# Routing of the later two token groups among the first expert's w_out products, six pieces by group at the end

## The chip, the cores and the metric

One core of a Trainium2 chip runs the whole program in one launch. The metric is device microseconds of one execution. Five engines work side by side, each through its own instructions in order: PE (TensorE, matmuls), ACT (ScalarE), DVE (VectorE), POOL (GpSimd) and SP (SyncE), which here issues nearly every transfer. PEld is the loading of the matmuls' fixed operand.

## The reference, cut to what matters

```python
x = attention(q, k, v, omega)                 # 1152 tokens x 512, random features
h = x @ w_in                                  # 2048 hidden channels
g = h * np.clip(h + 3.0, 0.0, 6.0) / 6.0
x = g @ w_out                                 # 1152 x 512
logits = x @ w_gate                           # 8 experts
expert_idx = np.argmax(logits, axis=1)
...                                           # softmax; a token counts if its expert has had < 288 before it
h = np.maximum(np.einsum('ecd,edf->ecf', disp, w1), 0.0)
y = np.einsum('ecf,efd->ecd', h, w2)
out[i] = gate_w[i] * y[expert_idx[i], pos[i]] # for the tokens that are kept, else 0
```

q, k and the weights of the middle layer are float64 or float32 of random numbers; the result is 1152 x 512 float32.

## The kernel before

After the attention the tokens stand in three groups of 384 (g = 0, 1, 2) and the 2048 hidden channels in 16 pieces of 128 (f = 0 to 15). PE makes `h` for one piece and one group with 12 matmuls (`hidden_in`, L274); ACT and DVE make `g` of it (L278, L282), in one of eight buffers with the tag `g`; SP stores it to memory (`gall`, and `gfirst` for group 0).

The logits are not made from `g @ w_out`. For each f, `w_out` is multiplied by `w_gate` first (`fold_gate`: four transposes, L296, four matmuls, L303, and ACT's copy to `wog`, L306), and `logits` (L315) adds `wog` times `g` into one PSUM bank `lg`, one matmul for each group. The constant `TAIL` says for how many of the last f this goes by group: all of group 0 of those f comes first, then groups 1 and 2, so that the logits of group 0 end early.

Routing has two parts: p = 0 is group 0, p = 1 is groups 1 and 2. Its steps, by the planner's names: `lc` (ACT copies the logits, L328), `lt` (PE turns them, L337, L340), `best` (DVE, eight small operations, L386 to L405), `exp` (ACT, L410), `rk` (PE, ranks within each expert, L416 to L420), `kept` (DVE, L426 to L449), `cb` (PE, sums over tokens, L474), `cc` (DVE, eleven small operations, L477 to L508: which expert e, and from which token s on, a window of 288 consecutive tokens is to serve), `gate` (DVE, L455 to L459). SP then reads s (L511) and e (L513) into registers and waits for DVE at that, with all later transfers behind it in its queue. `Lm` stores the rows `meta` of expert and weight to memory (`mfirst`, `mall`; L464, L465: 8 bytes for each token), and `Lsm` loads the rows of a window back (L545).

The first choice serves one window of the first group and one expert, the second another window over all tokens; a last branch serves what would be left. For each window: 16 loads of `g` at the chosen token (`gw`, L541, 144 KB each, in the same eight buffers), a split of each into two halves (`gh` on ACT, L549, `gl` on DVE, L551: the remainder; four buffers), and 16 products with `w_out` (`Yw`, L558, 12 matmuls each, into four PSUM banks). The sum is split into two halves (`th`, ACT, L568, and `tl`, DVE, L570: tile `dT`). Then the expert: eight loads of its weights (L590 for w1, L593 for w2: `rawe`, 512 KB each, four buffers), each for two splits (weight splits `wsplit`: `u`, ACT, L603; the remainder `v`, DVE or POOL, L605), eight products with w1 (`h0`, L626), products with w2, and the rows to the output.

The order on every engine is made by a planner (`Plan.order`): each step has an engine, a cost, what it comes after, which buffers it takes and frees, and a rank; the planner goes through time and gives each engine the step of lowest rank that could start. The program is then written in that order, and each engine keeps to it. Costs and ranks change nothing but this order. A wait on the chip is only one for data or for a buffer; of SP's transfers at most eight are under way, since the ninth waits for the first.

Of the kernel before, what the change touches and what calls it, by code (L numbers as in the profile page):

```python
# [10 lines left out]
F32 = mybir.dt.float32  # L11
# [120 lines left out]
def moe_kernel(ctx, tc, q, k, v, v_rest, omega, w_in, w_out, w_gate, w1, w2, out, cap):  # L132
# [6 lines left out]
    E, F2 = w2.shape[0], w2.shape[1]  # L139
    KD = DM // 128  # L140
    NG = 3
# [7 lines left out]
    F2T = F2 // 128  # L149
    F1T = FF // 128  # L150
# [10 lines left out]
    GB = 8  # L161
    WO0 = 4
# [3 lines left out]

    AHEAD = 4

    TAIL = 4
    H_TP = (1, 3, 5, 7)  # L170
    SPLITS = ["PDPDPDPDPDPDPDPD", "PDPDPDPDPDPDPDPD"]
    ABS_FROM = 12
# [11 lines left out]
    wa = ctx.enter_context(tc.tile_pool(name="wa", bufs=7))  # L184
    wo0 = ctx.enter_context(tc.tile_pool(name="wo0", bufs=WO0))
# [104 lines left out]
    wog = {}  # L290

    def fold_gate(f):
        wo = wtile["o", f].bitcast(F32)
        tp = pt.tile([128, KD, 128], F32, tag="tp", name="tpW")
        for kk in range(KD):
            nc.tensor.transpose(tp[:, kk, :], wo[:, kk * 128:(kk + 1) * 128], ident)  # L296
        yield
        woT = late_pools["woT"].tile([128, KD, 128], F32, tag="woT", name="woT")
        nc.scalar.activation(out=woT, in_=tp, func=ACTF.Copy)
        yield  # L300
        ps_ = late_pools["ac2"].tile([128, E], F32, tag="ac2", name="wogp")
        for kk in range(KD):
            nc.tensor.matmul(ps_, lhsT=woT[:, kk, :], rhs=wg[:, kk, :], start=(kk == 0), stop=(kk == KD - 1))  # L303
        yield
        wog[f] = late_pools["woT"].tile([128, E], F32, tag="wog", bufs=4, name="wog")
        nc.scalar.activation(out=wog[f], in_=ps_, func=ACTF.Copy)  # L306


    lg = []
# [16 lines left out]
    def logits_out(g):  # L326
        ps = slice(32 * g, 32 * g + E)
        nc.scalar.activation(out=lgT[0][ps], in_=lg[0][ps], func=ACTF.Copy)  # L328
# [3 lines left out]
    def turn_logits(p):  # L332

        lgr[p] = late_pools["ac2"].tile([128, len(PARTS[p]), E], F32, tag="ac2", name="lgr")
        if p == 0:
            for c in range(TPG):
                nc.tensor.transpose(lgr[p][:, c, :], lgT[0][0:E, c * 128:(c + 1) * 128], ident[0:E, 0:E])  # L337
            return
        for c in range(TPG):
            nc.tensor.matmul(  # L340
                lgr[p][:, c::TPG, :], lhsT=lgT[0][:, c * 128:(c + 1) * 128],
                rhs=ident.rearrange("p (g e) -> p g e", e=32)[:, 1:NG, 0:E], start=True, stop=True,
            )
# [524 lines left out]
    def turn_out(u):  # L868
# [31 lines left out]

    plan = Plan(dict(
        tp=4, pj=2, acc=1, x=XB, phi=3, phiR=1, phT=2, xo=2, nm=4, rd=4, x32=X32, raww=4, rawx=RAWX, rawv=2,
        t=2, g=GB, wa=7, wo0=WO0, wo=F1T - WO0 + 1, ohi=F1T, woT=2, wog=4, gh=4, wb=F2T - 1, g6k=2 * NG, yT2=2, lg=1, ac2=1,
    ), HOP, AGAIN, INTO, SLACK)

    def rank(stage, u):
# [41 lines left out]
    for u, (nm, b, c, hh) in enumerate(seq):  # L948
# [15 lines left out]
        for z in range(2):  # L964
# [4 lines left out]
                    after=[f"N{z}{u}"] + [f"P0{u}"] * z, takes=None if z else "phiR" if is_r else "phi",  # L969
                    frees=[f"B{z}{u}", f"N{z}{u}"], rank=rank("P", u))),  # L970
# [5 lines left out]
        after=[f"P0{ur}", f"P1{ur}", "VvR"] + [f"KR{x - 1}"] * (x > 0), takes="tp", frees=[f"P0{ur}"], rank=rank("K", ur))) for x in range(3)])  # L976
    chain(gen, [(f"KT{x}", "ACT", 0.46 if x < 2 else 0.37, dict(after=[f"KR{x}"] + [f"KT{x - 1}"] * (x > 0), frees=[f"KR{x}"], rank=rank("KV", ur))) for x in range(3)])
    for b in range(B):
        kus = [units["k", b, c, hh] for c in range(2) for hh in range(2)]
        names = []  # L980
        for u in kus:
            _, _, c, hh = seq[u]
            for z in range(2):
                name = f"K{b}.{u}.{z}"
# [3 lines left out]
                    after=[f"P{z}{u}", f"Vv{b}{c}"] + names[-1:], frees=[f"P0{u}"] + ([f"Lv{b}{c}"] if hh == 1 else []), rank=rank("K", u),  # L988
                    takes=None if names else "acc",
# [8 lines left out]
    for u, (nm, b, c, hh) in enumerate(seq):  # L998
        if nm != "q":
            continue  # L1000
        for z in range(2):
# [3 lines left out]
                    after=[f"C{z}{u}"] + [f"T0{u}"] * z, takes=None if z else "phT", frees=[f"C{z}{u}"], rank=rank("T", u))),  # L1005
            ])
        for z in range(2):
            chain(attend(u, z), [
                (f"D{z}{u}", "PE", 0.856, dict(
                    after=[f"T{z}{u}"] + [f"KV{bb}" for bb in range(B) if b in (bb, "R")], takes="tp",  # L1010
                    frees=[f"T0{u}"], rank=rank("D", u))),
# [11 lines left out]
    late_pools = {}  # L1023
# [37 lines left out]
    def load2(name, fn, cost, latency=0.95, **kw):  # L1061
        plan.add("L" + name, "SP", cost, fn, **kw)
        plan.add("V" + name, "in" + name, latency, lambda: None, after=["L" + name])
# [62 lines left out]
    for n, (_, f, g) in enumerate(order):  # L1126
        me = f"{f}.{g}"
        tag = "tp" if n % 2 else "pj"
# [15 lines left out]
    for f in range(F1T):  # L1144
        for gs in ([(0, 1, 2)] if f < F1T - TAIL else [(0,), (1, 2)]):
            plan.add(f"L{f}.{gs[0]}", "PE", 0.75, lambda a=(f, gs): logits(*a), after=[f"Hg{f}.{g}" for g in gs] + [f"Gc{f}o"] + ([] if first else ["L0.0"]),
                     takes="lg" if first else None, frees=[f"Hg{f}.{g}" for g in gs] + ([f"Gc{f}o"] if gs[-1] == NG - 1 else []), rank=pe_rank["L", f, gs[-1]])
# [3 lines left out]
        plan.named[f"L{f}.1"]["after"].append("lc0")  # L1151
    plan.add("lz", "Pool", 0.5, clear_logits, after=[f"WLi{F1T - 1}"], takes="x32", rank=0.0)
    for g in range(NG):
        plan.add(f"lc{g}", "ACT", 0.57, lambda g=g: logits_out(g), after=["lz", f"L{F1T - 1}.{min(g, 1)}"], frees=["L0.0"] if g else [], rank=-850)
    for p in range(2):
        plan.add(f"lt{p}", "PE", 0.2 if p else 0.1, lambda p=p: turn_logits(p), after=["lc1", "lc2"] if p else ["lc0"], takes="ac2", frees=["lz"] if p else [], rank=-800)


    for p in range(2):
        T = len(PARTS[p])  # L1160
        r = -800
        run_of(f"best{p}", route_best(p), [(0.1, [f"lt{p}"])] + [(0.094,), (0.094,), (0.094, 1), (0.094, 2), (0.094,), (0.094,), (0.081,)], r)
        plan.named[f"best{p}.0"]["frees"].append(f"lt{p}")
        plan.add(f"exp{p}", "ACT", 0.15, lambda p=p: route_exp(p), after=[f"best{p}.3"], rank=r)
        plan.add(f"rk{p}", "PE", 0.2 if p else 0.1, lambda p=p: route_rank(p), after=[f"best{p}.7"] + (["kept0.7"] if p else []), takes="ac2", rank=r)
        run_of(f"kept{p}", route_kept(p), [(0.094, [f"rk{p}"]), (0.094,), (0.07,), (0.07, 1), (0.094, 2), (0.094, 3), (0.07, 2)] + ([(0.094, None)] if not p else []), r)
        plan.named[f"kept{p}.0"]["frees"].append(f"rk{p}")
        gen = choose(p)
        chain(gen, [(f"cb{p}", "PE", 0.12, dict(after=[f"kept{p}.5"] + ([] if not p else ["cb0"]), takes="ac2", rank=r))])
        ops = [(0.1, [f"cb{p}"])] + [(0.08,)] * (9 + 2 * p)  # L1170
        run_of(f"cc{p}", gen, ops, r)
        plan.named[f"cc{p}.0"]["frees"].append(f"cb{p}")
        last = f"cc{p}.{len(ops) - 1}"
        chain(gen, [
            (f"cs{p}", "SP", 0.55, dict(after=[last], rank=-2000)),
            (f"ce{p}", "SP", 0.55, dict(after=[f"cs{p}"], rank=-1990 if p else -1950)),
        ])
        if p == 0:
            chain(gen, [("ct0", "DVE", 0.08, dict(after=[last], then=[last], rank=r))])
        run_of(f"gate{p}", route_gate(p), [(0.094, [f"exp{p}"]), (0.07,), (0.08,)], r + 50)  # L1180
        load2(f"m{p}", lambda p=p: save_meta(p), 0.5, 2.0, after=[f"gate{p}.2", f"kept{p}.6"], rank=-1940)
# [7 lines left out]
    for x, f in enumerate(YORDER):  # L1189
        prev = YORDER[x - 1]  # L1190
# [5 lines left out]
    def add_window(p, r):  # L1196
        x = windows[p]

        def load_meta():
            x.start = chosen[p]["st"]  # L1200
            x.load_meta()

        load2(f"sm{p}", load_meta, 0.5, 2.0, after=[f"cs{p}", f"Vm{p}"] + ([] if not p else ["Vm0"]), rank=-1930)
        run_of(f"to{p}", experts[p].target(), [(0.07, [f"Vsm{p}"]), (0.07,), (0.08,)], r + 40)
        for n, f in enumerate(YORDER):
            prev = f"{p}.{n - 1}" if n else f"{p - 1}.{F1T - 1}" if p else ""
            stored = [f"VHs{f}.{g}" for g in range(NG if p else 1)]
            load2(f"gw{p}.{n}", lambda f=f: x.load(f), 0.45, 2.0, after=[f"cs{p}"] + stored, takes="g", rank=-1980 + n + 400 * p, then=["Lgw" + prev] if prev else [])
            chain(x.halve(f), [
                (f"gh{p}.{n}", "ACT", 0.41, dict(after=[f"Vgw{p}.{n}"], takes="gh", rank=r + n, then=["gh" + prev] if prev else [])),  # L1210
                (f"gl{p}.{n}", "DVE", 0.45, dict(after=[f"gh{p}.{n}"], frees=[f"Lgw{p}.{n}"], rank=r + n)),
            ])
            plan.add(f"Yw{p}.{n}", "PE", 1.62, lambda f=f: x.product(f), after=[f"gl{p}.{n}", f"ol{f}"] + ([f"Yw{p}.{n - 1}"] if n else []),
                     takes=None if n else [("tp", f"yw{p}.{kk}") for kk in range(KD)], frees=[f"gh{p}.{n}"], rank=r + n)
        for kk in range(KD):
            chain(x.tokens(kk), [
                (f"th{p}.{kk}", "ACT", 0.33, dict(after=[f"Yw{p}.{F1T - 1}"] + ([f"th{p}.0"] if kk else []),
                                                  takes=None if kk else [("g6k", f"d{p}0"), ("g6k", f"d{p}1")], rank=r - 200)),
                (f"tl{p}.{kk}", "DVE", 0.38, dict(after=[f"th{p}.{kk}"], frees=[f"yw{p}.{kk}"], rank=r - 200)),
            ])  # L1220
# [187 lines left out]
```

## Time and profile before

| | us |
|---|---|
| median of three runs | 346.6 (345.59 to 346.85) |
| the profiled execution | 347.02 |
| its span, first to last instruction | 345.2 |
| PE busy | 328.8 (95% of the span) |
| DVE busy | 225.7 (65%) |
| ACT busy | 180.2 (52%) |

All times within the program are microseconds from the start of the span. The profiled execution spends 1.8 us outside its span. [...]

### The profile page before, as it was taken

How to read it: one execution, taken by the hardware profiler on the slowest of the kernel's cores; microseconds unless marked ns; L12 is line 12 of the kernel's file. 1: busy time of each engine (PE TensorE's matmuls, PEld its weight loads, DVE VectorE, ACT ScalarE, POOL GpSimd, SP SyncE). 2: the span in 40 equal slices, each digit the busy share in tenths (PEclk: the TensorE clock that was granted, in tenths of full speed). 3: DMA queues.
4: the chain of work that ended last, by engine and by line, in shares of the span. 5: the costliest groups of instructions: out<-in, count | busy, mean ns of one | idle time of the engine just before them, and what ended most of it. 6: DMA issues, size and time to landing. Idle time of an engine off the chain costs nothing.

```text
span 345.2 us, 6458 instructions
## 1 busy us (share of the span) xinstructions
PE 328.8 (95%) x2307; PEld 300.8 (87%) x2307; DVE 225.7 (65%) x465; ACT 180.2 (52%) x436; POOL 76.7 (22%) x74
## 2 busy tenths in 40 slices
PE   8998999999999999999999999599989999999992
PEld 5998899999888888888888778399889989999782
DVE  5489999899889899988884436377676202654100
ACT  6987999973345545554374622325646232624110
POOL 0846543100112121122000000013604212511021
PEclk9999999999999999999999999969999999999998
DMA  7996921013666867676322211858746004710011
GB/s 253 357 316 255 356 102 63 2 52 142 214 210 217 259 232 253 235 269 217 114 92 104 91 59 49 246 112 252 249 121 244 2 0 131 252 65 0 4 46 30
DMA packets 29674, 54.06 MB, mean 157 GB/s; under 512 B 5537, under 2 KB 18209, under 8 KB 29633
## 3 DMA queue, kind: packets, MB, share of 16 engines
q1 hardware_dynamic: 29248, 52.38, 45.9%
q0 software_dynamic: 384, 1.18, 1.1%
q8 instruction: 20, 0.33, 0.4%
q14 instruction: 22, 0.17, 0.2%
HBM read 37.42 MB, written 16.13 MB: 155 GB/s over the span
## 4 chain that ended last, share of the span: by engine, by line
PE 79%; issue 8%; DMA 4%; DVE 4%; ACT 2%; SPq 1%; POOL 1%; POOLq 0%; ACTq 0%; DVEq 0%
PE hp L274 30%; PE yw L558 10%; PE pj L776 6%; PE hp L626 6%; PE lg L315 5%; PE wogp L303 4%; PE yq L648 4%; PE nd L847 4%; PE kvp L799 3%; PE tpW L296 2%; PE tpC L829 2%; DMA rawe<-in_w_dram 2%; DMA out_dram<-scratch,to 2%; DMA rawx<-in_k_dram 1%; PE tpE L872 1%
## 5 line engine op out<-in xcount | busy, mean ns | idle before, releaser
L274 PE MATMUL hp<-xT,wsplit 128*128 128x384 f32 x576 | 112.5, 343 | 0.0
L274 PEld LDWEIGHTS hp<-xT,wsplit 128*128 128x128 f32 x576 | 98.0, 188 | 9.7 <-issue 8.4
L278 ACT ACTIVATE t<-hp,three 128x384 f32<-128x384 f32 x48 | 27.8, 580 | 56.9 <-PE hp L274 53.5
L558 PE MATMUL yw<-gh,ohi 128*128 128x288 f32 x256 | 54.1, 304 | 1.2 <-DVE gh L551 1.1
L605 POOL TENSOR_TENSOR wsplit<-rawe,wsplit 128x512 fp32r<-128x512 f32 x16 | 22.4, 1403 | 108.8 <-ACT wsplit L603 104.4
L558 PEld LDWEIGHTS yw<-gh,ohi 128*128 128x128 f32 x256 | 42.6, 195 | 2.6 <-DVE gh L551 1.9
L788 ACT ACTIVATE phi<-pj,nm 128x128 f32<-128x128 f32 x144 | 40.6, 422 | 6.6 <-DVE nm L782 5.7
L261 POOL TENSOR_TENSOR wsplit<-x,wsplit 128x512 fp32r<-128x512 f32 x16 | 22.9, 1430 | 90.2 <-ACT wsplit L259 78.1
L282 DVE SCALAR_TENSOR_TENSOR g<-t,hp 128x384 f32<-128x384 f32 x48 | 26.5, 551 | 19.2 <-ACT t L278 19.0
L558 PE MATMUL yw<-gh,olo 128*128 128x288 f32 x128 | 38.6, 301 | 0.0
L551 DVE TENSOR_TENSOR gh<-gw,gh 128x288 fp32r<-128x288 f32 x32 | 19.6, 629 | 27.8 <-ACT gh L549 27.8
L782 DVE TENSOR_REDUCE nm<-pj 128x4 f32<-128x512 f32 x36 | 24.6, 685 | 5.1 <-PE pj L776 4.2
L766 POOL TENSOR_TENSOR xl<-rawx,xh 128x512 fp32r<-128x512 f32 x16 | 21.8, 1370 | 24.3 <-ACT xh L764 24.3
L776 PE MATMUL pj<-wbd,xh 128*128 128x256 f32 x144 | 25.9, 303 | 1.3 <-ACT phi L788 0.9
L626 PE MATMUL hp<-dT,wsplit 128*128 128x288 f32 x192 | 26.0, 295 | 0.8 <-ACT gh L549 0.8
L626 PEld LDWEIGHTS hp<-dT,wsplit 128*128 128x128 f32 x192 | 25.7, 188 | 0.8 <-ACT gh L549 0.8
L558 PEld LDWEIGHTS yw<-gh,olo 128*128 128x128 f32 x128 | 24.8, 194 | 0.0
L603 ACT ACTIVATE wsplit<-rawe 128x512 fp32r<-128x512 f32 x32 | 19.0, 623 | 10.5 <-DMA rawe<-in_w_dram 10.5
L549 ACT ACTIVATE gh<-gw 128x288 fp32r<-128x288 f32 x32 | 13.6, 437 | 17.3 <-PE yw L558 15.0
L776 PEld LDWEIGHTS pj<-wbd,xh 128*128 128x128 f32 x144 | 19.8, 193 | 2.9 <-ACT phi L788 1.4
L605 DVE TENSOR_TENSOR wsplit<-rawe,wsplit 128x512 fp32r<-128x512 f32 x16 | 17.4, 1086 | 4.5 <-ACT wsplit L603 4.4
L303 PEld LDWEIGHTS wogp<-wg,woT 128*128 128x128 f32 x128 | 16.3, 191 | 1.9 <-ACT t L278 1.9
(146 smaller groups left out, 503.9 us busy)
## 6 DMA issues: line engine op xcount, KB each, us to landing
gall<-g SPq DMA_DIRECT2D x48, 192.0 KB, 2.4
raw<-in_w_in_dram SPq DMA_DIRECT2D x16, 512.0 KB, 4.1
raw<-in_w_out_dram SPq DMA_DIRECT2D x16, 512.0 KB, 3.9
rawe<-in_w_dram SPq DMA_DIRECT2D x16, 512.0 KB, 5.1
gfirst<-g SPq DMA_DIRECT2D x16, 192.0 KB, 2.3
rawx<-in_q_dram SPq DMA_DIRECT2D x9, 256.0 KB, 6.0
out_dram<-blank SPq DMA_DIRECT2D x1, 2304.0 KB, 9.0
gw<-gfirst SPq DMA_DIRECT2D x16, 144.0 KB, 3.0
```

What stands on the lines that cost most here:

```text
L261: nc.gpsimd.tensor_tensor(out=t[:, 1, :], in0=xf, in1=t[:, 0, :].bitcast(F32), op=ALU.subtract)
L274: nc.tensor.matmul(hp, lhsT=w[:, a, wk], rhs=xT[g][b_][:, kk, :], start=(n == 0), stop=(n == 3 * KD - 1))
L278: nc.scalar.activation(out=t, in_=hp, func=ACTF.Relu, bias=three[:, 0:1])
L282: nc.vector.scalar_tensor_tensor(out=gv, in0=t, scalar=6.0, in1=hp, op0=ALU.min, op1=ALU.mult)
L303: nc.tensor.matmul(ps_, lhsT=woT[:, kk, :], rhs=wg[:, kk, :], start=(kk == 0), stop=(kk == KD - 1))
L558: nc.tensor.matmul(self.ps[kk], lhsT=wohalf[f][a][:, kk * 128:(kk + 1) * 128], rhs=self.gh[f][:, b_, :], start=(f == YORDER[0] and n == 0) ...
L605: engine.tensor_tensor(out=lo, in0=part, in1=hi.bitcast(F32), op=ALU.subtract)
L626: nc.tensor.matmul(hp, lhsT=self.w[0, f][:, a, kk * 128:(kk + 1) * 128], rhs=self.window.dT[b_][:, kk, :], start=(n == 0), stop=(n == 3 * ...
L766: (nc.gpsimd if u in X_POOL else nc.vector).tensor_tensor(out=lo[:, sl], in0=rawt[u][:, sl], in1=hi[:, sl].bitcast(F32), op=ALU.subtract)
L776: nc.tensor.matmul(pj[:, 2 * jj:2 * jj + 2, :], lhsT=a[:, j, :], rhs=w, start=(jj == 0 and n == 0), stop=(n == 2), skip_group_check=True,)
L782: nc.vector.tensor_reduce(out=nm, in_=pj, axis=AX.X, op=ALU.max, negate=True)
L788: nc.scalar.activation(out=phis[u][:, 4 * half + h, :], in_=pj[:, h, :], func=ACTF.Exp, bias=nm[:, h:h + 1])
```

## The change

Three things are altered. `TAIL` goes from 4 to 6, so pieces 10 and 11 are made by group too, and the buffers of `wog` from 4 to 7 so that those pieces' products can wait. The ranks of the second part's routing go from -850 and -800 to 102 and 104.5, which is the rank of the first window's products (100 to 115). And of the first window's loads, the planner may place only three ahead of the last piece's `g`, at a cost of 0.5 and 3.0 instead of 0.45 and 2.0.

```diff
-    TAIL = 4
+    TAIL = 6
...
-        wog[f] = late_pools["woT"].tile([128, E], F32, tag="wog", bufs=4, name="wog")
+        wog[f] = late_pools["woT"].tile([128, E], F32, tag="wog", bufs=7, name="wog")
...
     for g in range(NG):
-        plan.add(f"lc{g}", "ACT", 0.57, lambda g=g: logits_out(g), after=["lz", f"L{F1T - 1}.{min(g, 1)}"], frees=["L0.0"] if g else [], rank=-850)
+        plan.add(f"lc{g}", "ACT", 0.57, lambda g=g: logits_out(g), after=["lz", f"L{F1T - 1}.{min(g, 1)}"], frees=["L0.0"] if g else [], rank=102 if g else -850)
     for p in range(2):
-        plan.add(f"lt{p}", "PE", 0.2 if p else 0.1, lambda p=p: turn_logits(p), after=["lc1", "lc2"] if p else ["lc0"], takes="ac2", frees=["lz"] if p else [], rank=-800)
+        plan.add(f"lt{p}", "PE", 0.2 if p else 0.1, lambda p=p: turn_logits(p), after=["lc1", "lc2"] if p else ["lc0"], takes="ac2", frees=["lz"] if p else [], rank=104.5 if p else -800)
...
-        r = -800
+        r = -800 if p == 0 else 104.5
...
-            load2(f"gw{p}.{n}", lambda f=f: x.load(f), 0.45, 2.0, after=[f"cs{p}"] + stored, takes="g", rank=-1980 + n + 400 * p, then=["Lgw" + prev] if prev else [])
+            load2(f"gw{p}.{n}", lambda f=f: x.load(f), 0.5, 3.0, after=[f"cs{p}"] + stored + [f"Hg{F1T - 1}.{NG - 1}"] * (n >= 3), takes="g", rank=-1980 + n + 400 * p, then=["Lgw" + prev] if prev else [])
```

On PE, from the last logits (`lg`) to the first window's products (`yw`), before:

```order
L315 MATMUL lg<-g,wog 8x384 x4
L340 MATMUL lgr<-ident,scratch 128x2x8 x3
L416 LDWEIGHTS below
L416 MATMUL rk<-ohb_2916,below 128x48
L418 LDWEIGHTS ones
...
L420 MATMUL rk<-carry,ones 128x8
L474 MATMUL cp<-kf_2939,ones_86 128x96
L558 MATMUL yw<-gh,ohi 128x288 x2
L558 MATMUL yw<-gh,olo 128x288
```

The same place after:

```order
L315 MATMUL lg<-g,wog 8x384 x4
L558 MATMUL yw<-gh,ohi 128x288 x2
...
L340 MATMUL lgr<-ident,scratch 128x2x8 x3
L558 MATMUL yw<-gh,ohi 128x288 x2
...
L416 LDWEIGHTS below
L416 MATMUL rk<-ohb_3006,below 128x48
...
L420 MATMUL rk<-carry,ones 128x8
L558 MATMUL yw<-gh,ohi 128x288 x2
...
L474 MATMUL cp<-kf_3054,ones_86 128x96
L558 MATMUL yw<-gh,ohi 128x288 x2
```

The products now follow the logits at once; `lgr` stands after three of the sixteen, `rk` after five and `cp` after six.

On SP, from the store of the second part's `meta` on, before (L511 and L513 read s and e into registers):

```order
L465 DMA mall<-meta 128x6x2
...
L511 TENSOR_LOAD ei_2984
...
L590 DMA rawe<-in_w_dram 128x1024
L513 TENSOR_LOAD ei_2984
...
L541 DMA gw<-gfirst_127 128x288
...
L545 DMA sm<-mall 96x3x2
...
L590 DMA rawe<-in_w_dram 128x1024
...
L593 DMA rawe<-in_w_dram 128x2x512
```

After, where all sixteen loads `gw` of the first window and two weight loads stand ahead of this place:

```order
L511 TENSOR_LOAD ei_3111
...
L590 DMA rawe<-in_w_dram 128x1024
L513 TENSOR_LOAD ei_3111
...
L465 DMA mall<-meta 128x6x2
...
L590 DMA rawe<-in_w_dram 128x1024
...
L593 DMA rawe<-in_w_dram 128x2x512
...
L545 DMA sm<-mall 96x3x2
...
L593 DMA rawe<-in_w_dram 128x2x512
...
L541 DMA gw<-gall_103 128x288
```

Of the first expert's eight weight loads one stood ahead of the read of s, and now two do. `mall<-meta` has moved behind the reads, with two weight loads between it and `sm<-mall`, which reads what it stores; two more weight loads and the second window's first load `gw<-gall` follow `sm` (before, eight loads and the reads lay between the two).

On ACT, ahead of the split of the window's sum (`dT`), before and after (`wsplit` is a weight split, `gh` one of `g`):

```order
L603 ACTIVATE wsplit<-rawe 128x512
L549 ACTIVATE gh<-gw 128x288 x4
L568 ACTIVATE dT<-yw 128x288 x4
```

```order
L603 ACTIVATE wsplit<-rawe 128x512 x6
L549 ACTIVATE gh<-gw 128x288
L568 ACTIVATE dT<-yw 128x288 x4
```

Before, four splits of `g` stand between the last weight split and `dT`; after, one, which is the first of the second window.

## Rows read from the trace of the kernel before

**Rows 1.** PE in order of time: start, length, instruction [idle before, what ended it].

```profile
220.33 0.84 PE L340 MATMUL lgr<-ident,scratch 128*128 128x16 f32 x6 [1.06 <-ACT scratch L328]
223.02 0.20 PE L416 MATMUL rk<-ohb,below 128*128 128x48 bf16 x1 [1.84 <-DVE ohb L405]
...
223.18 0.30 PE L420 MATMUL rk<-carry,ones 128*128 128x8 bf16 x6
224.67 0.72 PE L474 MATMUL cp<-kf,ones 128*128 128x96 f32 x2 [1.19 <-DVE kf L443]
225.09 0.83 PE L558 MATMUL yw<-gh,ohi 128*128 128x288 f32 x2
...
230.11 0.43 PE L558 MATMUL yw<-gh,ohi 128*128 128x288 f32 x2
...
248.23 0.30 PE L558 MATMUL yw<-gh,olo 128*128 128x288 f32 x1
...
254.55 0.18 PE L1054 MATMUL lp<-leftb,ones 128*128 128x1 bf16 x1
255.52 4.76 PE L626 MATMUL hp<-dT,wsplit 128*128 128x288 f32 x34 [0.80 <-ACT gh L549]
```

**Rows 2.** Stretches: from:to, length, busy (count) of PE, PEld, DVE, ACT, POOL, PEclk, DMA, GB/s.

```profile
34.00:36.00 2.00, 0.76 (x5) 0.53 (x5) 1.93 (x6) 1.41 (x5) 1.08 (x1) 1.00 0.70 272
219.30:223.30 4.00, 1.12 (x17) 1.03 (x18) 1.82 (x10) 2.64 (x7) 0.00 (x0) 1.00 0.88 218
225.10:230.10 5.00, 4.82 (x20) 4.47 (x20) 4.36 (x16) 1.05 (x3) 1.28 (x1) 0.50 0.52 31
230.10:234.00 3.90, 3.90 (x31) 3.90 (x31) 1.88 (x9) 1.60 (x4) 0.45 (x1) 1.00 0.85 273
```

**Rows 3.** The chain that ended last, in order of time: start, length, what.

```profile
167.07 0.79 PE wogp L303 x8
...
187.56 0.76 PE lg L315 x6
188.32 0.99 PE wogp L303 x8
...
191.88 0.74 PE lg L315 x2
...
217.20 2.09 PE lg L315 x8
```

**Rows 4.** DVE in order of time: the second part's `cc`, two remainders of `g`.

```profile
225.42 0.26 DVE L477 TENSOR_REDUCE tot<-cp 128x16 f32<-128x96 f32 x1 [0.39 <-PE cp L474]
225.72 0.86 DVE L481 TENSOR_TENSOR tot<-tot,tot 128x16 f32<-128x16 f32 x1
...
228.17 0.15 DVE L508 CAST ei<-st 128x1 int32<-128x1 f32 x1
...
231.63 0.46 DVE L551 TENSOR_TENSOR gh<-gw,gh 128x288 fp32r<-128x288 f32 x1 [0.65 <-ACT gh L549]
...
243.15 1.37 DVE L551 TENSOR_TENSOR gh<-gw,gh 128x288 fp32r<-128x288 f32 x1 [1.12 <-ACT gh L549]
```

**Rows 5.** SP's transfers in order of time, around the read of s at L511.

```profile
224.73 0.39 SPq L465 DMA_DIRECT2D mall<-meta  x1
...
229.11 0.35 SPq L590 DMA_DIRECT2D rawe<-in_w_dram  x1
230.28 0.90 SPq L541 DMA_DIRECT2D gw<-gfirst  x2
```

**Rows 6.** The page's transfers: count, KB each, median us from issue to landing.

```profile
mall<-meta SPq DMA_DIRECT2D x1, 6.0 KB, 4.7
```

**Rows 7.** The weight tile `rawe`, 205 to 262 us, and ACT's splits.

```profile
DMA to landing us min/median/max: 3.7/4.5/6.6
```

**Rows 8.** ACT in order of time: a pair of weight splits, a split of `g`.

```profile
224.56 1.15 ACT L603 ACTIVATE wsplit<-rawe 128x512 fp32r<-128x512 f32 x2 [2.14 <-DMA rawe<-in_w_dram]
...
238.91 0.43 ACT L549 ACTIVATE gh<-gw 128x288 fp32r<-128x288 f32 x1
```

More of the change, by code (lines that the diff above doesn't have):

```diff
@@ L902, in moe_kernel @@
         tp=4, pj=2, acc=1, x=XB, phi=3, phiR=1, phT=2, xo=2, nm=4, rd=4, x32=X32, raww=4, rawx=RAWX, rawv=2,
-        t=2, g=GB, wa=7, wo0=WO0, wo=F1T - WO0 + 1, ohi=F1T, woT=2, wog=4, gh=4, wb=F2T - 1, g6k=2 * NG, yT2=2, lg=1, ac2=1,
+        t=2, g=GB, wa=7, wo0=WO0, wo=F1T - WO0 + 1, ohi=F1T, woT=2, wog=7, gh=4, wb=F2T - 1, g6k=2 * NG, yT2=2, lg=1, ac2=1,
     ), HOP, AGAIN, INTO, SLACK)
```

## The prediction

> **What bounds the kernel now.** I read PE's timeline first, since the other engines either feed it or wait for it. The last logits (eight matmuls, [rows 3]) end at 217.20 + 2.09 = 219.29. Then PE has little to do until 225.09: `lgr` after 1.06 idle, `rk` after 1.84, `cp` after 1.19, each wait ended by ACT or DVE [rows 1]. That is the second part's routing: 5.80 us with nothing beside it. The stretches, read next, show a second price. PE is busy 1.12 of 4.00 us, and then the granted clock is 0.50, until about 230.1 [rows 2]. In the 5.02 us of products at that level (225.09 to 230.11) 18 matmuls run. At clock 1.00, from 230.11 to 248.23, 137 take 18.12 us, 0.132 each [rows 1]; 18 would take 2.38. After the last product (`lp` at 254.55) the first expert's products begin at 255.52, 0.97 later [rows 1]. So from the last logits to the expert it is 36.23 us, and of these 16 x 12 x 0.132 = 25.4 are products at full clock.
>
> **Six pieces by group.** Pieces 10 and 11 each lose a joint logits step of 0.76 and get two instead. One group alone takes 0.74 [rows 3], since the groups of one step run beside each other; two take something between, so I add 2 x 0.73 = 1.46. Two more `wogp` steps follow logits instead of a piece, 0.99 instead of 0.79 [rows 3]: 0.40. PE has no gap in this stage, so all of it is on the path; a few tenths may come back, as pieces follow each other directly in places. I take **+1.8**, bounds +1.4 and +2.0. The logits then end at 221.1. In return the first choice is made some 8 us earlier (the two groups of two more pieces now follow it), and its window's first three loads can land and be split before the last logits. The larger `wog` costs no time: its copies are the same. The planner's new cost of the loads moves them in SP's queue only: after the third they stand behind the stores of piece 15, from about 218 on, and the fourth product does not begin before 225.
>
> **Routing among the products.** The 5.80 us go, and the routing's work on PE comes back between products: `lgr` 0.84, `rk` 0.46 (223.02 to 223.48), `cp` 0.4 to 0.7 (0.72 at the lower clock) [rows 1]: 1.8 in all. With no idle there is no fall of the clock, and the 2.64 us that 18 slow matmuls lose go too. Three waits take the place of the old ones. `lgr` comes after three products (4.75 us); ACT's copies were done 1.06 after the logits [rows 1], so it doesn't wait. `rk` comes two products (3.2 us) after `lgr`, and DVE needs 1.85 between them (221.17 to 223.02): no wait. `cp` comes one product after `rk`, at 231.9. DVE has two remainders of `g`, a weight split and a third remainder ahead of `kept`. A remainder takes 0.46 or, in the longest row shown, 1.37 [rows 4]; a weight split has 512 columns to its 288, so I estimate 0.8. They end at 231.0, and `kept` takes 1.2 (the wait of 1.19): `cp` at 232.2, a wait of 0.3, bounds 0 and 1.5. Behind it stand only products. If all loads come in time, the products end at 221.1 + 25.4 + 1.8 + 0.3 = 248.6 or a little before, and with the 0.97 seen now the expert begins at 249.3: 6.2 us earlier.
>
> **SP and the weights.** What changes most off PE is when s is known, because SP waits for it with six weight loads and the second window's loads behind. DVE begins `cc` after `cp`, the rest of `kept`, a remainder and a weight split, at 233.4, and needs 2.25 (225.42 to 228.32, less 0.65 of an operation of the length of the others that took 0.86): s is there at 235.6, where it was at 228.32 [rows 4]. The transfer behind a read went 0.79 after it, the next 1.17 after that (229.11 and 230.28, [rows 5]). So the third weight load goes at 236.4, `mall<-meta` at 237.6. `sm` reads what that stores and waits until it has landed; the one such store in the page took 4.7 [rows 6], so 242.3. Before, eight loads lay between the two and hid this. Only then, at 242.9 and 243.5, come two more weight loads. Weights took 3.7 to 6.6 to land, median 4.5 [rows 7]; with another close ahead of it I take 5.1 for the last: 248.6. ACT does its splits in order: the last two weights (1.15, [rows 8]) until 249.8, the second window's first `gh` (0.43) until 250.2, and behind them `dT`. DVE follows with a weight split, a remainder and its half of `dT` (0.8, 0.46 and another 0.46): 251.8. The expert begins at **252.0**, 3.5 us earlier than now. With 3.7 for the landing it is 250.6, with 6.6 and one disturbed operation on DVE 254.4.
>
> All that follows keeps its order relative to that product, and the second window's loads have 30 us. So the profiled execution goes from 347.02 to 343.5, and the median of 346.6, which is 0.4 below it, to **343.1**.
>
> **The clock in that gap.** PE then stands for about 3 us between 249 and 252. The rows show both outcomes of a pause: with 1.24 idle in 2.00 us (34 to 36) the clock stayed at 1.00; with 2.88 idle in 4.00 us it was 0.50 afterwards [rows 2]. This gap lies nearer the second. [...]
>
> **Rivals.**
>
> *Loads in time.* If `mall<-meta` lands sooner than 4.7 or the last weights take 3.7, and DVE is not disturbed, ACT is hardly late and the gap shrinks towards the 0.97 of now: -6.2, **340.4**. For it: the 4.7 is a single transfer. Against: `sm` and two weights stand behind it whatever it takes.
>
> *Late and slow.* The gap is there and the clock falls as after 223.3. By the rows that costs up to 2.6 us (5.02 against 2.38 for 18 products): -3.5 + 2.6 = -0.9, **345.7**.
>
> *Slower than before.* A weight split on DVE stands ahead of `cc`, and it needs the second weight load, which is issued at about 222.2 behind seven loads of `g`. If that lands later than 231.4, each microsecond pushes s and all loads behind it by one. From 234.9 on the kernel is slower than now; at 237 it is +2, **348.7**. Against: it would be 13 us under way, twice the longest landing shown [rows 7].
>
> *Routing not hidden.* DVE is always late, and PE waits between its products the 1.06 + 1.84 + 1.19 = 4.1 us as now [rows 1]. The late weights would be covered by that in part: about -1.0, **345.6**.
>
> **How the numbers follow.** Forecast 0.45; loads in time 0.22; late and slow 0.20; not hidden 0.07; slower 0.06. The range, 340.2 to 345.7, reaches from loads in time to late and slow and leaves out the slower case and the outer parts of those two. A measurement of this kernel tells about 0.5% (1.7 us) from no change. Faster by more: nearly all of the forecast (0.42), loads in time (0.22), a fifth of late and slow (0.04), 0.68 in all. Slower by more: the slower case and 0.02 of the others, 0.08. Within: 0.24.
>
> **What the profile after would show.** The last logits end at 221.1 and the next product follows without idle; the clock is 1.00 to the end of the products; `lgr`, `rk` and `cp` stand among them with tenths of idle; s is read at 235.6; weight loads go at 236.4 and, behind a wait for `mall<-meta`, at 242.9; a gap of some 3 us precedes the expert's first product at 252.0, and ACT or DVE ends it. The forecast is wrong if that product begins before 250.6 or after 253.5, or if the clock is 0.50 around it.

## The result, and the profile after

The changed kernel takes 349.0 us (median of 16 executions, 347.13 to 352.13), the kernel before 346.6 in the same runs. The ratio is 1.0067 with a 95% interval of 1.0038 to 1.0097: it is 0.7% slower, where 343.1 was forecast. The profiled execution took 350.02 and its span 348.3. In the run s_dve below two of the twelve executions were disturbed (457 and 1123 us): the ratio there leaves them out, the median does not.

PE of the changed kernel, in the columns of [rows 1]:

```profile
218.50 2.14 PE L315 MATMUL lg<-g,wog 128*8 128x384 f32 x8
220.58 0.54 PE L558 MATMUL yw<-gh,ohi 128*128 128x288 f32 x2
...
225.48 0.74 PE L340 MATMUL lgr<-ident,scratch 128*128 128x16 f32 x6
...
232.98 0.43 PE L474 MATMUL cp<-kf,ones 128*128 128x96 f32 x2 [1.46 <-DVE meta L445]
...
247.41 0.40 PE L558 MATMUL yw<-gh,ohi 128*128 128x288 f32 x1 [1.14 <-ACT gh L549]
248.80 0.40 PE L558 MATMUL yw<-gh,ohi 128*128 128x288 f32 x1 [0.99 <-DVE gh L551]
...
251.97 0.18 PE L1054 MATMUL lp<-leftb,ones 128*128 128x1 bf16 x1
255.37 15.76 PE L626 MATMUL hp<-dT,wsplit 128*128 128x288 f32 x96 [3.22 <-DVE gh L551]
270.97 6.56 PE L648 MATMUL yq<-h,wsplit 128*128 128x288 f32 x48
```

The first half is what the change was to do. The products follow the logits at once, and `lgr` stands among them without idle time. Then PE waits three times among the products (1.46, 1.14, 0.99; in the kernel before it was 0.18, 0.68 and 0.21), and 3.22 us ahead of the first expert. That expert begins at 255.37, where it was 255.52 [rows 1], and its 96 products with w1 last 15.60 to the next line's start, where they lasted 12.87 (255.52 to 268.39). The stretches tell why, in the columns of [rows 2]:

```profile
240.00:242.00 2.00, 2.00 (x17) 2.00 (x16) 0.00 (x0) 0.44 (x1) 0.00 (x0) 1.00 1.29 66
...
252.00:255.30 3.30, 0.15 (x3) 0.07 (x1) 3.23 (x8) 1.43 (x5) 1.03 (x1) 0.91 0.13 47
255.40:258.00 2.60, 2.60 (x11) 2.60 (x12) 2.32 (x7) 1.11 (x3) 0.00 (x0) 0.50 0.24 64
...
260.00:262.00 2.00, 2.00 (x12) 2.00 (x11) 0.33 (x2) 0.41 (x1) 0.00 (x0) 0.62 0.85 253
262.00:264.00 2.00, 2.00 (x17) 2.00 (x16) 0.79 (x2) 0.41 (x1) 0.00 (x0) 1.00 0.99 359
```

After the pause the granted clock (PEclk, a share of full speed) is 0.50 until about 261.5, as it was after the routing's pause before [rows 2]. The slow stretch has not gone, it has moved from the products to the expert. SP and ACT show what is late:

```profile
221.19 0.86 SPq L590 DMA_DIRECT2D rawe<-in_w_dram  x2
...
236.80 0.33 SPq L590 DMA_DIRECT2D rawe<-in_w_dram  x1
237.77 0.40 SPq L465 DMA_DIRECT2D mall<-meta  x1
238.37 0.78 SPq L590 DMA_DIRECT2D rawe<-in_w_dram  x1
239.40 0.38 SPq L593 DMA_DIRECT2D rawe<-in_w_dram  x1
242.62 0.33 SPq L545 DMA_DIRECT2D sm<-mall  x1
243.21 1.41 SPq L593 DMA_DIRECT2D rawe<-in_w_dram  x2
```

```profile
241.56 1.15 ACT L603 ACTIVATE wsplit<-rawe 128x512 fp32r<-128x512 f32 x2 [2.84 <-DMA rawe<-in_w_dram]
...
246.40 0.63 ACT L603 ACTIVATE wsplit<-rawe 128x512 fp32r<-128x512 f32 x1 [3.35 <-DMA rawe<-in_w_dram]
246.93 0.76 ACT L549 ACTIVATE gh<-gw 128x288 fp32r<-128x288 f32 x2
...
250.63 1.15 ACT L603 ACTIVATE wsplit<-rawe 128x512 fp32r<-128x512 f32 x2 [0.31 <-DMA rawe<-in_w_dram]
```

ACT's split at 246.40 waits 3.35 us for the fourth weight load (issued 238.37), and behind it in ACT's order stand two splits of `g`, without which PE cannot go on: that is the 1.14 at 247.41. The last weight was there at 250.63. DVE and POOL in the same columns, DVE first:

```profile
229.77 1.77 DVE L605 TENSOR_TENSOR wsplit<-rawe,wsplit 128x512 fp32r<-128x512 f32 x1
...
233.19 0.68 DVE L605 TENSOR_TENSOR wsplit<-rawe,wsplit 128x512 fp32r<-128x512 f32 x1
...
247.39 2.82 DVE L551 TENSOR_TENSOR gh<-gw,gh 128x288 fp32r<-128x288 f32 x2 [2.18 <-ACT gh L549]
250.13 1.78 DVE L605 TENSOR_TENSOR wsplit<-rawe,wsplit 128x512 fp32r<-128x512 f32 x1
251.83 1.23 DVE L613 TENSOR_SCALAR tok<-slotidx,st 96x3 f32<-96x3 f32 x1
...
254.64 0.15 DVE L1057 CAST lefti<-lp 128x1 int32<-128x1 f32 x1
254.71 0.45 DVE L551 TENSOR_TENSOR gh<-gw,gh 128x288 fp32r<-128x288 f32 x1
255.07 1.54 DVE L570 SCALAR_TENSOR_TENSOR dT<-yw,dT 128x288 fp32r<-128x288 f32 x4
```

```profile
228.06 2.93 POOL L605 TENSOR_TENSOR wsplit<-rawe,wsplit 128x512 fp32r<-128x512 f32 x2 [64.52 <-ACT wsplit L603]
...
247.16 5.88 POOL L605 TENSOR_TENSOR wsplit<-rawe,wsplit 128x512 fp32r<-128x512 f32 x4 [3.59 <-ACT wsplit L603]
```

A weight split takes DVE 0.68 alone, but 1.77 and 1.78 while POOL is at work; three columns on 96 partitions take 1.23. So DVE is late too: its half of `dT` begins at 255.07, though ACT's was ready from 252.5 on.

What ends the pause is neither half of `dT`. Ahead of the expert every engine reads the value of the test for a last branch, `lefti`, into a register (L1059), and DVE makes that value with the cast at 254.64, behind its late splits. The read in TensorE's stream, with its length in ns and its start:

```profile
L1059 PEldq TENSOR_LOAD <-lefti x1: 490/490/490, 254.8 to 254.8; - x1
```

The expert begins 0.58 us after the end of the cast (254.79 and 255.37). It does so in the kernel before as well (254.94 and 255.52), and 0.58 to 0.59 after it in six of the runs below: pieces, routing, nogw, s_weights, s_dve and s_split (in s_meta and s_both `dT` comes later still).

### The profile page after: what moved, and what is told of

The parts are those of the page before. It is cut to its first block, busy times and chain, and to the rows that moved or that the text cites. A ratio compares the mean times of both kernels' runs of the same rounds, so it can differ in the third digit from the quotient of the medians.

```text
span 348.3 us, 6457 instructions
## 1 busy us (share of the span) xinstructions
PE 331.3 (95%) x2307; PEld 301.8 (87%) x2307; DVE 226.5 (65%) x465; ACT 179.4 (52%) x436; POOL 77.0 (22%) x74
## 3 DMA queue, kind: packets, MB, share of 16 engines
q0 software_dynamic: 384, 1.18, 1.1%
## 4 chain that ended last, share of the span: by engine, by line
PE 75%; issue 8%; DMA 7%; DVE 6%; SPq 1%; ACT 1%; POOL 1%; POOLq 0%; DVEq 0%; ACTq 0%
PE hp L274 30%; PE yw L558 9%; PE hp L626 6%; PE pj L776 5%; PE lg L315 5%; PE wogp L303 4%; PE yq L648 4%; PE nd L847 4%; DMA rawe<-in_w_dram 2%; PE tpW L296 2%; PE kvp L799 2%; DMA raw<-in_w_in_dram 2%; PE tpC L829 2%; DMA out_dram<-scratch,to 2%; DVE wsplit L605 1%
## 5 line engine op out<-in xcount | busy, mean ns | idle before, releaser
L558 PE MATMUL yw<-gh,ohi 128*128 128x288 f32 x256 | 52.7, 299 | 2.3 <-ACT gh L549 1.1
L558 PEld LDWEIGHTS yw<-gh,ohi 128*128 128x128 f32 x256 | 41.2, 189 | 4.1 <-DVE gh L551 1.4
L558 PE MATMUL yw<-gh,olo 128*128 128x288 f32 x128 | 37.9, 296 | 0.0
L626 PE MATMUL hp<-dT,wsplit 128*128 128x288 f32 x192 | 28.7, 315 | 3.2 <-DVE gh L551 3.2
L626 PEld LDWEIGHTS hp<-dT,wsplit 128*128 128x128 f32 x192 | 28.4, 207 | 3.3 <-issue 3.3
L558 PEld LDWEIGHTS yw<-gh,olo 128*128 128x128 f32 x128 | 24.1, 188 | 0.0
```

Of the source, the lines that this page charges most:

```text
L558: nc.tensor.matmul(self.ps[kk], lhsT=wohalf[f][a][:, kk * 128:(kk + 1) * 128], rhs=self.gh[f][:, b_, :], start=(f == YORDER[0] and n == 0) ...
L626: nc.tensor.matmul(hp, lhsT=self.w[0, f][:, a, kk * 128:(kk + 1) * 128], rhs=self.window.dT[b_][:, kk, :], start=(n == 0), stop=(n == 3 * ...
```

## The experiments

Each ratio is to the kernel before in the same runs. The first three runs take the change apart.

**pieces**: only `TAIL` and the buffers of `wog`.

> The first part of the change alone: pieces 10 and 11 by group and the larger wog; the routing's ranks and the loads as before. My theory: the pieces cost what the changed kernel shows, a last logits end 1.35 us later (220.64 against 219.29), and the routing then costs its idle time and the half clock as before, so about 1.4 us more than before: 348.0. Rival (the pieces are the whole loss): 349.0 or more, with the first expert's products at 257.5 or later. Second rival (the earlier first choice gives something back, because weights come early): at most 346.6.

Measured: 346.1, ratio 0.9969 (0.9942 to 0.9996), a little faster. The price of the pieces is as forecast: from the start of the first product with w_in to the end of the last it is 143.55 us, before 141.76 (+1.79). But with the window's loads in hand earlier the planner put products ahead of `lgr` here too, with the ranks of before, so a part of the routing was hidden already; the expert began at 254.55. Its products wait too (0.93 and 1.02), and behind these waits the granted clock is 0.50 (244 to 246): a product takes 0.24 there and 0.13 from 247.2 on. The second rival had the value; early weights, its reason, are not what the order shows.

**routing**: only the three ranks; `TAIL` is 4.

```diff
-... frees=["L0.0"] if g else [], rank=-850)
+... frees=["L0.0"] if g else [], rank=102 if g else -850)
-... frees=["lz"] if p else [], rank=-800)
+... frees=["lz"] if p else [], rank=104.5 if p else -800)
-        r = -800
+        r = -800 if p == 0 else 104.5
```

> The second part of the change alone: the later groups' routing at the rank of the products, four pieces by group and the rule for the loads as before. In this program three weight loads of the first expert stand ahead of the store of the second part's meta rows and of the read of s, where the changed kernel has them behind the read. My theory (routing among products gains, late weights give it away): products follow the logits at 219.3, no weight is late, the first expert's products begin at 247.5 to 249.5 with the clock at 1.00: 339.5 to 341.5. Rival (the routing among products itself is what loses, by DVE being late for it): products wait 4 us in all, 344 to 346.

Measured: 343.1, ratio 0.9908 (0.9875 to 0.9941): the gain is real and needs only this part. From the last logits to the expert it is 32.5 us (218.08 to 250.57), 3.7 less than before. The size lies between the two theories, since waits of 1.04, 0.63, 1.00 and 1.56 remain.

**nogw**: the changed kernel without its third part.

```diff
-... x.load(f), 0.5, 3.0, after=[f"cs{p}"] + stored + [f"Hg{F1T - 1}.{NG - 1}"] * (n >= 3), ...
+... x.load(f), 0.45, 2.0, after=[f"cs{p}"] + stored, ...
```

> The changed kernel without the new rule and cost for the window's loads: six pieces by group and the routing among the products. SP has three weight loads ahead of the read of s. My theory: as in the routing's change alone, with logits that end 1.35 us later: 341 to 343, the expert at 249 to 251 and no fall of the clock. Rival (six pieces and the routing together lose): 348 to 350 as the changed kernel.

Measured: 348.8, ratio 1.0057 (1.0033 to 1.0081): my theory fell, as far as it put the late weights down to the third part. Two parts, each faster than before (by 0.3% and 0.9%), are slower together. SP of this kernel:

```profile
230.19 0.33 SPq L590 DMA_DIRECT2D rawe<-in_w_dram  x1
230.76 0.38 SPq L593 DMA_DIRECT2D rawe<-in_w_dram  x1
239.58 0.40 SPq L465 DMA_DIRECT2D mall<-meta  x1
240.23 1.59 SPq L593 DMA_DIRECT2D rawe<-in_w_dram  x2
```

Its loads of `g` are through sooner, SP comes to the read of s at 231 and stands there for 7.7 us, with the store of `meta` and two weight loads behind it. In the run routing the first of these two had gone at 234.81, ahead of the read. PE of nogw waits twice among its last products, and behind that the granted clock is 0.50:

```profile
249.03 0.40 PE L558 MATMUL yw<-gh,ohi 128*128 128x288 f32 x1 [1.18 <-ACT gh L549]
251.51 0.61 PE L558 MATMUL yw<-gh,ohi 128*128 128x288 f32 x1 [2.08 <-DVE gh L551]
...
252.00:254.00 2.00, 2.00 (x10) 2.00 (x10) 1.93 (x7) 0.99 (x3) 0.00 (x0) 0.50 0.28 74
```

Its expert begins at 255.34, as in the changed kernel, and takes 12.86 for the 96 products. So the question became what the queue behind that read costs. The next runs keep the changed kernel's order on every engine and move a few steps by name, the ones in brackets ahead of the one behind them (`Le0` is a weight load of the first expert, `Lgw` a load of `g`, `v` a remainder of weights, `Lm`, `Lsm` and `to` are the meta rows' store, load and use, `cc1.11` is the read of s). **s_weights**:

```diff
     steps = plan.order()
+    move(['Le0.02', 'Le0.03'], 'Lgw0.10')
+    move(['Le0.10', 'Le0.11'], 'cc1.11')
```

> The changed kernel in its own order, but on SP two of the first expert's weight loads (the third and fourth) stand ahead of the tenth load of g and two more (the fifth and sixth) ahead of the read of s, so that only one of the seven is still behind the meta rows. Theory (weights late behind the read of s): ACT's weight splits no longer hold up a split of g, the products lose their waits of 1.14 and 0.99, and the first expert's products begin at 250.5 to 252.5 with the clock at 1.00: 343 to 345.5. Rival (DVE's own work is what is late, the weights only follow it): products end at 251 to 252, the gap stays at about 3 us: 347.5 to 349.

Measured: 343.0, ratio 0.9892 (0.9861 to 0.9922): 6.0 us less than the changed kernel from four moved transfers. PE:

```profile
250.60 13.13 PE L626 MATMUL hp<-dT,wsplit 128*128 128x288 f32 x96 [1.25 <-DVE gh L551]
263.56 6.58 PE L648 MATMUL yq<-h,wsplit 128*128 128x288 f32 x48
```

The waits of 1.14 and 0.99 are gone, the gap is 1.25 and the expert's 96 products last 12.96 (12.87 in the kernel before, at clock 1.00): no fall of the clock. The wait at `cp` (1.47) stays, since it is DVE's. With these moves the whole change is as fast as its ranks alone (343.1 in the run routing).

**s_meta**: the meta rows out of the weights' way.

```diff
+    move(['to1.0', 'to1.1', 'to1.2'], 'hl0.3')
+    move(['Lm1'], 'Lgw1.0')
+    move(['Lsm1'], 'Lgw1.6')
```

> The changed kernel in its own order, but the store of the second part's meta rows (8 bytes each) stands behind the weight loads, their load back behind six loads of the second window, and what DVE makes of them after the fourth product of the expert. Theory (these rows hold SP's queue for 2.6 us and the weights' transfer beside them): four weight loads go within 3 us of the read of s, the last lands by 247, and the products end some 2 us earlier: 344 to 346.5. Rival (the weights wait for each other anyway, and DVE for its own work): 348 to 349.

Measured: 346.4, ratio 1.0002 (0.9976 to 1.0027), 2.6 less than the changed kernel, at the upper end of what I expected. The products end at 249.46, 2.7 earlier, but the gap is still 2.64, and the 96 products behind it last 14.70 (12.96 in s_weights), which I put down to the clock. There ACT ends it: its split of the second window's first `g`, ahead of `dT`, waits 2.29 for the load, until 251.19.

**s_both**: both remedies.

> The changed kernel with both remedies at once: four weight loads earlier (as in s_weights) and the meta rows later (as in s_meta). If the two remedies act on one cause, weights that land late, the sum is no larger than the larger of them: 342 to 343.5. If they are two causes that add up (6.0 and 2.6 less than the changed kernel): 340 to 341.

Measured: 343.4, ratio 0.9913 (0.9879 to 0.9947): no more than s_weights alone. The two act on one cause, weights that land late.

**s_dve**: DVE's order ahead of the expert.

```diff
+    move(['v0.11', 'to1.0', 'to1.1', 'to1.2', 'v0.13', 'v0.15', 'gl1.0'], 'gl1.1')
```

> The changed kernel in its own order, but on DVE three weight splits of w2, the target rows and the second window's first remainder stand behind its half of dT and the cast for the branch, not ahead of them. Loads and ACT as in the changed kernel. Theory (at the gap it is DVE's order that is late, not the weights): products still end at 252.1, the expert begins at 252.8 instead of 255.4 and the clock stays at 1.00 (2.7 less): 343.7 to 345. Rival (the waits at 246 to 249 already bring the clock down): the expert begins at 252.8 but its products take over 15 us: 346 to 347. Second rival (weights for the first expert's product are missing): 349.

Measured: 348.8, ratio 1.0044 (1.0021 to 1.0067): no gain to speak of, though the expert begins at 252.61, as expected, with 0.80 idle. PE now waits 0.89 and 0.60 for `h` at 266.80 and 270.19, and over the ten executions the clock differs (0.984 to 0.997). The splits that were put off are not to blame, they are done by 256.4. What is late is the eighth weight load, issued at 259.23 (259.71 in the changed kernel), and behind its split stand ACT's and DVE's steps for `h`:

```profile
263.82 1.16 ACT L603 ACTIVATE wsplit<-rawe 128x512 fp32r<-128x512 f32 x2 [3.86 <-DMA rawe<-in_w_dram]
```

An expert that begins 2.8 us earlier meets the next late weight. The two waits take back 1.5 of these 2.8; the rest was not taken apart.

**s_split**: four of the first expert's splits on DVE instead of POOL.

```diff
-... x.halve(kind, f, nc.vector if where == "D" else nc.gpsimd)
+... x.halve(kind, f, nc.vector if where == "D" or k == 0 and n in (6, 8, 10, 12) else nc.gpsimd)
```

> The changed kernel in its own order, but four of the first expert's weight splits that GpSimd made (one of w1, three of w2) are made by VectorE. In the changed kernel VectorE's operations that run beside GpSimd's splits take far longer than alone (a weight split 1.78 instead of 0.68 at 250.13, 1.23 instead of 0.22 at 251.83, two remainders 2.82 instead of 0.83 at 247.39). Theory (they wait for GpSimd): four more splits of 0.68 on VectorE cost 2.7 us and the stretched ones give 4 us back, the expert begins at 254 to 255: 347 to 348.5. Rival (the stretching has another cause): VectorE is 2.7 us later, the expert begins at 257 to 258: 350 to 352.

Measured: 346.5, ratio 0.9986 (0.9961 to 1.0010), 2.5 less than the changed kernel with 2.7 us more work on DVE. DVE there:

```profile
248.47 0.82 DVE L551 TENSOR_TENSOR gh<-gw,gh 128x288 fp32r<-128x288 f32 x2
...
250.41 0.22 DVE L613 TENSOR_SCALAR tok<-slotidx,st 96x3 f32<-96x3 f32 x1
```

The same two remainders take 0.82 instead of 2.82, the target row 0.22 instead of 1.23, and the gap is 0.80. The weights land no sooner. PE still waits 1.32 and 0.42 among the last products, and in this execution the clock falls there instead of in the gap:

```profile
250.00:252.00 2.00, 2.00 (x10) 2.00 (x10) 1.93 (x6) 1.81 (x4) 0.00 (x0) 0.50 1.07 371
```

**s_fill** and **s_fill2** are on the clock: 24 matmuls that nobody reads, in the gap.

```diff
+    def fill():
+        ps_ = late_pools["lg"].tile([128, cap], F32, tag="lg", name="fp")
+        for n in range(24):
+            w = wohalf[YORDER[n % F1T]][0]
+            nc.tensor.matmul(ps_, lhsT=w[:, 0:128], rhs=w[:, 128:128 + cap], start=True, stop=True)
```

> The changed kernel in its own order, with 24 matmuls of 128x288 that nobody reads put on TensorE between the last product of the first window and the first expert's products, where it stood idle for 3.22 us. My theory (the clock's fall is a price of its own): the expert still begins at 255.4, its 96 products take 13.0 instead of 15.76 us: 2.7 us less than the changed kernel, 346.3. Rival (the clock falls from the earlier waits at 246 to 249, or the fall is not what makes the products long): 349.0, no change.

Measured: 351.4, ratio 1.0140 (1.0100 to 1.0181), slower still. I had overlooked that every engine reads the branch value `lefti` (L1059) and that the filling stood behind this read on PE. So it began only after DVE's cast, and at a granted clock of 0.64 from 254.4 to 259, and put the expert 3.8 us later:

```profile
254.40 4.91 PE L1293 MATMUL fp<-ohi 128*128 128x288 f32 x24 [3.23 <-DVE gh L551]
259.15 12.94 PE L626 MATMUL hp<-dT,wsplit 128*128 128x288 f32 x96
```

> The 24 idle-time matmuls of the run s_fill again, now ahead of the read of the branch value on TensorE and so directly behind the last product, where in s_fill they stood behind that read and did not begin before 254.4. Theory (the clock falls in the gap of 3.2 us, and keeping TensorE at work holds it): the filling runs from 252.1 to 255.3 at clock 1.00, the expert begins at 255.4 to 256 and its 96 products take 13.0 us: 346.3 to 347. Rival (the clock has fallen by the waits among the products): 349 or more.

Measured: 348.1, ratio 1.0049 (1.0030 to 1.0068), 0.9 less than the changed kernel. In the profiled execution it did what was expected:

```profile
252.28 3.41 PE L1293 MATMUL fp<-ohi 128*128 128x288 f32 x24
255.67 13.13 PE L626 MATMUL hp<-dT,wsplit 128*128 128x288 f32 x96
268.63 6.56 PE L648 MATMUL yq<-h,wsplit 128*128 128x288 f32 x48
```

With PE at work the clock stays at 1.00 (252.4 to 260) and the 96 products last 12.96. The waits among the products are there too (1.20 and 0.98); in pieces, nogw and s_split the clock was 0.50 behind waits at this place, here and in the changed kernel it was 1.00 behind them. That the median gains 0.9 and not 2.7 fits the spread of the changed kernel: its mean granted clock over 16 executions goes from 0.986 to 0.996, with spans from 350.4 down to 345.4, so the fall is not as deep in each; in s_fill2 eight of twelve stand at 0.996 or 0.997. Even the changed kernel's four executions at 0.995 and above have spans of 345.4 to 345.9, and the median of before less the 1.8 outside the span is 344.8: without the clock's fall the change would still bring nothing.

**best1** is the run routing with what the other runs point to.

```diff
+    move(['Le0.02', 'Le0.03'], 'Lgw0.10')
+    move(['Le0.10', 'Le0.11'], 'Lgw0.15')
+    move(['Le0.12'], 'cc1.11')
+    move(['lc1', 'lc2'], 'gh0.4')
+    move(['to1.0', 'to1.1', 'to1.2'], 'hl0.3')
+    move(['Lm1'], 'Lgw1.0')
+    move(['Lsm1'], 'Lgw1.6')
+    move(['zm'], 'h0.3')
+    move(['zi'], 'hl0.3')
+    move(['zl'], 'h0.6')
```

Here `lc` and `gh` are steps of ACT, `h` one of PE and `hl` one of DVE in the expert, and `zm`, `zi` and `zl` are the sum, the cast and the read for the last branch.

> Four pieces by group and the routing among the products (as in the run routing), with the repairs that the other runs point to: four weight loads stand ahead of the last loads of g and a fifth ahead of the read of s; the meta rows are stored behind the read and loaded back behind six loads of the second window; ACT splits the window's first four loads ahead of its copies of the logits; the test for a last branch and its read stand among the expert's products. Theory: the product follows the logits within 0.5, the last products have no wait, the gap before the expert is under 1 us: about 8 us from the last logits to the expert less than before, 338 to 340. Rival (VectorE is the bound of this stretch): the gap stays at 1.5 and products wait 1 to 2 us: 342 to 343, as the run routing.

Measured: 342.9, ratio 0.9889 (0.9857 to 0.9921), the rival's value: no better than the run routing. With the weights in time and the read of the branch value among the expert's products, PE waits for DVE (0.67, 0.91, 1.09, 1.01).

**best2** takes POOL out of this stretch as well.

```diff
-    move(['Le0.12'], 'cc1.11')
+    move(['v0.04', 'v0.05', 'v0.06'], 'gl0.11')
-... x.halve(kind, f, nc.vector if where == "D" else nc.gpsimd)
+... x.halve(kind, f, nc.vector if where == "D" or k == 0 and n < 14 else nc.gpsimd)
```

> The run best1 with all weight splits of w1 and the first six of w2 of the first expert on VectorE instead of half of them on GpSimd, and three of them behind the choice of the second window there. In best1 VectorE is what TensorE waits for among the products (0.67, 0.91, 1.09, 1.01 and 0.31), and seven of its operations run beside GpSimd's splits, 6.4 us longer than alone. Theory (VectorE's wait for GpSimd is what is left): seven more splits cost 4.8 us of VectorE's time and free 6.4, the choice comes sooner, and TensorE's waits fall from 4.0 to about 2.5: 341 to 342. Rival (the work itself is what is left): no change or worse, 343 to 344.5.

Measured: 340.2, ratio 0.9807 (0.9778 to 0.9836), the best of all, and below what I expected. The products run from 218.85 to 246.85 with a single wait of 0.49, and the expert begins 0.50 after them:

```profile
247.35 5.41 PE L626 MATMUL hp<-dT,wsplit 128*128 128x288 f32 x36 [0.50 <-ACT dT L568]
252.60 0.18 PE L1054 MATMUL lp<-leftb,ones 128*128 128x1 bf16 x1
252.64 8.23 PE L626 MATMUL hp<-dT,wsplit 128*128 128x288 f32 x60
```

How much of this is the engine of the splits and how much their order was not taken apart.

## Why the prediction was wrong

| step | forecast | measured |
|---|---|---|
| last logits end | 221.1 | 220.6 |
| wait at `cp` | 0.3 | 1.46 |
| third weight load | 236.4 | 236.8 |
| `mall<-meta`, `sm<-mall` | 237.6, 242.3 | 237.8, 242.6 |
| the load behind it | 242.9 | 243.2 |
| last weight there | 248.6 | 250.6 |
| products end | 248.6 | 252.1 |
| expert begins | 252.0 | 255.4 |
| its clock | 1.00 | 0.50 to about 261.5 |

The price of the pieces was right (1.79 for +1.8 in the run pieces; in the changed kernel the logits end 1.35 later), and so was the order of events on SP, each transfer within 0.4 us. The mechanism that I named, s read late and the weights behind it, is the one that decides: s_weights takes it away and gives 343.0. What it costs was wrong in four places; the first is a step that failed, the others are terms that were mis-sized or put at nothing.

- *"If all loads come in time, the products end at 221.1 + 25.4 + 1.8 + 0.3 = 248.6"*. *"ACT does its splits in order"* stands in the prediction too, but I let that order cost time only after the products. The splits of `g` for the last two products stand behind a weight split as well, so the products themselves waited (1.14 and, on DVE, 0.99). s_weights has neither wait; s_split, with four of POOL's splits on DVE, leaves 0.42 of the second. This step failed outright: the products end 3.5 later than forecast, 2.1 of it here and 1.2 at `cp`.
- *"With another close ahead of it I take 5.1 for the last."* Landings had a median of 5.9 and went up to 8.3:

```profile
DMA to landing us min/median/max: 4.0/5.9/8.3
```

  The two of 8 us were under way with the rows of `meta`. In the table of stretches the DMA column stands at 1.29 at 240 to 242, with 66 GB/s. In s_meta, with the rows behind them, the same two loads land after 4.8 and 6.2. Moving the rows gave 2.6 us in all; how much of it is SP's wait and how much the shared transfer was not taken apart.
- *"A remainder takes 0.46 or, in the longest row shown, 1.37"*, booked as an accident. The 1.37 of [rows 4] is no accident: POOL's split ran from 242.92 to 244.21 beside it, and the remainder ended 0.31 after that split. In the changed kernel the first three of the four operations ahead of `kept` run beside two of POOL's splits (228.06 to 230.99) and take 3.7 instead of 1.7, which is the wait at `cp`, and DVE is the engine that ends the gap. s_split and best2 show it. There the prediction also names the wrong end: *"a weight split, a remainder and its half of `dT`"* leaves out the target rows, two more weight splits and the cast, and PE waits for the read of that cast and not for `dT`. No run moves the read alone.
- *The clock in that gap.* I put 0.20 on the fall and took the other side as likeliest. The gap was 3.22 long and the clock 0.50 behind it: 2.73 us. s_fill2, with work in the gap, stays at 1.00.

In the profiled execution the expert is 3.4 later than forecast, and from there to the end of the span it is 92.9 where it was 89.7 [rows 1]: 2.7 of these 3.2 are the clock. Together 6.6, but for 0.1 outside the span the 350.0 against my 343.5. The rival *late and slow* had the right shape but took the rest of the forecast as it was, and the range ended at 345.7 because no case let the products be late as well as the gap. What this says of the change as a whole: the 5.8 us of routing were hidden but for the 1.46 at `cp`, but under them the weights had had time to come. The seventh of their loads had gone by 241.8 before and by 244.6 after, so with products that end earlier it is the weights that set the end, at about the same time as before.

## What to carry over

When a wait is taken out of the bound engine, work out when the next thing comes that used to be covered by it, down the whole queue: here SP stood 3.7 us at its read of a register value, ahead of transfers that had nothing to do with it, and moving four of them took 6.0 us off the changed kernel, more than the ranks alone had gained (3.4). An in-order engine that serves two streams (here splits of weights and of `g`) makes the urgent one wait for the late one, so a late transfer costs not only its own consumer: ACT waited 3.35 us for a weight, and PE 1.14 for the split of `g` behind it. And two changes that each gain can lose together: measure them apart before they are put in one.

## What the runs showed of the hardware

DVE's operations took longer beside POOL's splits. In the run routing, `L492` on 128x8 took 1.21 (0.23 otherwise) and ended with POOL's split of 235.81 to 237.10; in best1, seven operations of DVE beside POOL's splits took 6.4 us longer than alone, more than the 4.8 us of seven splits at the 0.68 that DVE takes for one. This goes down to operations of 0.2 us. What lies behind it, no run shows.

The read of a branch value stands in TensorE's own order. In s_fill, matmuls that needed nothing waited 3.23 us behind it and began 0.59 us after the end of DVE's cast; in s_fill2, ahead of the read, the same matmuls began at once. The wait carries the name of a DVE instruction in the profile, with nothing to say that it is the read.

How much time the clock spends below 1.00 is not the same in each execution of one program: the changed kernel's mean granted clock goes from 0.986 to 0.996. In the profiled executions it fell behind one pause of 3.22 us (the changed kernel), behind two of 1.18 and 2.08 (nogw) and behind two of 1.32 and 0.42 (s_split), and it did not behind two of 1.20 and 0.98 (s_fill2).
